# The end of a fused attention and expert kernel: where the last group's sums are read, and where the closing products stand

## The chip, the cores and the metric

The kernel runs on one core of one Trainium2 chip. A core has five engines that run side by side and wait for each other through semaphores: TensorE (PE; its weight loads are shown apart as PEld), VectorE (DVE), ScalarE (ACT), GpSimd (POOL), and SyncE (SP), which issues DMAs. PE multiplies into PSUM, eight banks of 128 partitions x 512 floats; DVE and ACT read and write PSUM and SBUF; POOL works in SBUF alone. The metric is the device time of one launch in microseconds (us), lower is better.

## The reference

Two blocks follow each other. The first is an attention with polynomial features: with `phi(x)` the 64 products of two 8-wide projections of `x`,

```python
kv  = einsum('bhsf,bhsd->bhfd', phi(k), v);  z = sum(phi(k), axis=2)
out = einsum('bhsf,bhfd->bhsd', phi(q), kv) / (einsum('bhsf,bhf->bhs', phi(q), z) + 1e-6)
```

Its result, as 4352 tokens of width 128, is `x` of the second block, a layer of eight experts with Sinkhorn routing:

```python
P = exp(x @ w_gate - max)                 # 4352 x 8
for _ in range(8):                        # rows, then columns, then N / E
    P /= P.sum(1); P /= P.sum(0); P *= N / E
for e in range(8):
    out += P[:, e:e+1] * (relu(x @ w1[e]) @ w2[e])   # w1: 128 x 1024, w2: 1024 x 128
```

Everything is in 32-bit floats.

## The kernel before

The attention and the routing take the first part of the span; most of the rest are the experts' two products. They are computed on 64x64 blocks with seven products in place of eight for each 2x2 block product, so that a weight tile of PE is 64x64 and four of them lie in the array at once: two row halves (`r`, where the input lies) by two column halves (`s`, where the output goes). The weight of a token is multiplied into its input ahead of the first product, which is allowed because it is positive and the Relu lets it through.

**Tokens and units.** The first 256 tokens (`REST`) are handled by themselves. The other 4096 are eight groups of 512 (`wgroups`, line 929). Seven experts by eight groups are 56 items (`witems`), each of two halves of the hidden width: 112 units (`units`). A unit has, for each row half, seven first products (`first_product`, line 1082), copies, sums and the Relu on ACT and DVE (`taps`, `hsums`), and seven second products, the tasks 0 to 6 of `second_products` (line 1123). Two records of the profile make one 64-wide matmul instruction, and a task has two such instructions, one for each `s`.

**The sums.** A group's second products add up over its seven experts in four PSUM banks, `ysums[g][0..3]`, tiles `s`. Bank `2 * r` holds two pieces of 256 columns, slots 0 and 1; bank `2 * r + 1` holds slots 2 and 3. Tasks 0 and 1 write slot 0, tasks 2 and 3 slot 1, tasks 4 and 5 slot 2, task 6 slot 3. For the last unit the tasks run in the order 6, 0, 4, 5, 1, 2, 3 (line 1321): banks 1 and 3 are complete first, then slot 0 of banks 0 and 2, and slot 1 last. What this file calls the two-piece bank is bank 0, read by the copy of line 1227.

**The order of the work** is written out by hand. `weighted_events` (line 1288) gives every instruction of this part a key, `b` plus an offset with `b = 14 * k` for unit `k`; the calls are made in the order of the keys, and each engine runs its own instructions in that order. Waits follow from which tile an instruction reads or writes. A PSUM tile is tracked as a whole: a write to one half of a bank waits for an earlier read of the other half.

**The last group's sums** (`last_end`, line 1204) are formed in 21 steps with the offsets `LAST_AT` (line 1202), behind unit 111, the last one. Steps 0 and 1 copy bank 1 to SBUF on ACT and add bank 3 on DVE; steps 2 and 3 move halves to the other partitions on ACT (lines 1220, 1221); steps 4 to 8 are DVE additions. Step 9 copies slot 0 of bank 0 (line 1227, ACT), step 10 adds slot 0 of bank 2 (DVE), steps 11 and 12 move halves (lines 1229, 1230, ACT), steps 13 to 16 are DVE additions, 17 and 18 add the slots 1 of banks 0 and 2 straight from PSUM. Step 19 transposes (line 1282, DVE) and step 20 stores (line 759, two DMAs from SP and two from POOL). All DVE additions have the line of the helper, 1216.

**The closing products** are the last expert's for the first 256 tokens, unsplit in the row direction: a weight tile of 128 rows by 64 columns (`128*64` in the profile, against `64*64`). `closing_first` (line 1180) makes the hidden part `c` of eight: two matmul instructions into bank `fbanks[c % 3]`, then a Relu on ACT (line 1185). `closing_second` (line 1187) makes one half `b` of 128 tokens of the output: an identity product that brings in what the other experts gave (`c = -1`), then eight products. `closing_out` (line 1195) copies the half to SBUF on ACT and issues four stores, two from SP and two from ACT. In the kernel before, `CLOSING_AT` (line 1167) puts the parts 0 to 3 at the offsets 24, 27, 30 and 33, among the second products of unit 110, and 4 to 7 behind everything of the last unit; both halves of the output use one bank, `fbanks[3]`.

```python
    LAST_AT = (42.1, 42.6, 42.7, 42.8, 43, 43.1, 43.2, 43.3, 43.4, 44.1, 44.6, 44.7, 44.8, 44.9, 45, 45.1, 45.2, 47.1, 47.6, 48.1, 48.2)
...
                for n, key in enumerate(CLOSING_AT):
                    at(b + key, closing_first, n)
                for n in range(2):
                    for c in range(-1, FO):
                        at(b + 49 + n, closing_second, n, c)
                    at(b + 49 + n, closing_out, n)
```

## Time and profile before

| what | value |
|---|---|
| timed runs, median of 3 | 909.7 us (908.74 to 910.84) |
| profiled execution | 907.8 us |
| its span, first to last instruction | 905.8 us |
| mean granted clock of PE | 0.995 |
| PE busy | 896.1 us of the span |
| first of the records of line 1183 | 880.3 us |
| copy of bank 1 (line 1218) starts | 887.71 us |
| last copy to SBUF (second line 1197) starts | 902.26 us |

In a timeline row stand the start in us, the busy time, the engine (a q behind it: its sequencer, as for a DMA issue), the line, the operation, what is written and read, the shape, the number of records, and in brackets the idle time of that engine just before and who ended it. A row of merged records lasts from the start of its first to the end of its last. In a chain row stand start, length, engine, tile, line and count. The granted clock is the share of PE's full speed that it was allowed; records take twice as long at 0.50. Matmul records overlap, since several tiles lie in the array at once.

### The profile page before, as it was taken

Reading aid. Unit: us, or ns where it says so; the run is one execution under the profiler, and the core shown is the slowest. Engines: PE = TensorE matmul, PEld = TensorE weight load, DVE = VectorE, ACT = ScalarE, POOL = GpSimd, SP = SyncE. Lnnn points to the kernel's source line nnn. Section 1 sums busy time; section 2 is a strip of 40 time slices with the busy share of each in tenths; the row PEclk is TensorE's granted clock in tenths of the full one; section 3 lists DMA queues with packets and bytes.
Section 4 is the critical chain, followed back from the end, with each engine's and each line's share of the span. In section 5 each row is a group of like instructions: output and inputs, shape, how many; then the busy total and the mean of one; then the engine's idle time right before and its main releaser. Section 6 shows DMA issues by size and latency. Waiting matters only on the chain.

```text
span 905.8 us, 34686 instructions
## 1 busy us (share of the span) xinstructions
PE 896.1 (99%) x14680; PEld 720.3 (80%) x14680; DVE 744.0 (82%) x1170; ACT 527.7 (58%) x1281; POOL 362.3 (40%) x373
## 2 busy tenths in 40 slices
PE   9999999999999999999999999999999999999997
PEld 6786667688787777788789998888888888878874
DVE  8667678968988988899898878887997898888862
ACT  3353456466566665665666566666656665666652
POOL 3013310042443535465763455354435443643310
PEclk9999999999999999999999999999999999999998
DMA  9998492235568877777886677787767777776710
GB/s 261 311 269 263 148 321 79 65 141 145 179 217 255 234 194 221 210 228 223 232 238 200 199 216 215 213 233 219 211 186 218 224 204 221 222 229 187 220 53 18
DMA packets 149498, 183.97 MB, mean 203 GB/s; under 512 B 15392, under 2 KB 111664, under 8 KB 148960
## 3 DMA queue, kind: packets, MB, share of 16 engines
q1 hardware_dynamic: 144048, 164.24, 62.0%
q0 software_dynamic: 4960, 17.42, 5.6%
q8 instruction: 116, 1.90, 0.8%
q14 instruction: 38, 0.31, 0.1%
q10 hardware_dynamic: 336, 0.10, 0.0%
HBM read 148.38 MB, written 18.65 MB: 184 GB/s over the span
## 4 chain that ended last, share of the span: by engine, by line
PE 95%; DVE 3%; issue 1%; ACT 1%; DMA 1%; SPq 0%; POOL 0%; ACTq 0%; DVEq 0%; POOLq 0%
PE a L1086 37%; PE s L1136 36%; PE a L789 8%; PE s L853 7%; PE a L371 1%; PE s L868 1%; PE a L486 1%; PE a L119 1%; PE a L1183 1%; PE a L1190 0%; PE a L338 0%; DVE hb L1115 0%; PE s L400 0%; PE a L450 0%; DVE hb L1121 0%
## 5 line engine op out<-in xcount | busy, mean ns | idle before, releaser
L1086 PE MATMUL a<-wb,w1f 64*64 64x256 f32 x4144 | 430.9, 377 | 0.4
L1086 PEld LDWEIGHTS a<-wb,w1f 64*64 64x64 f32 x4144 | 271.4, 133 | 36.2 <-issue 3.2
L1086 PE MATMUL a<-xf,w1f 64*64 64x256 f32 x2128 | 230.4, 377 | 0.3 <-DVE ht L1107 0.3
L1100 ACT COPY a<-a 128x256 f32<-128x256 f32 x224 | 80.0, 357 | 213.4 <-PE a L1086 213.4
L1136 PE MATMUL s<-hb,w2r 64*64 64x256 f32 x1344 | 191.2, 379 | 2.5 <-ACT wb L1227 2.1
L1136 PE MATMUL s<-ht,w2r 64*64 64x256 f32 x1344 | 190.4, 376 | 0.0
L201 POOL TENSOR_TENSOR wb<-wb 128x256 f32<-128x256 f32 (+1 forms) x115 | 131.0, 1141 | 118.7 <-DMA wb<-wb 91.8
L1136 PE MATMUL s<-ht,w2f 64*64 64x256 f32 x1216 | 159.5, 376 | 0.0
L1136 PE MATMUL s<-hb,w2f 64*64 64x256 f32 x1216 | 158.8, 377 | 0.0
L1086 PEld LDWEIGHTS a<-xf,w1f 64*64 64x64 f32 x2128 | 142.9, 133 | 18.5 <-issue 1.3
L1136 PEld LDWEIGHTS s<-hb,w2r 64*64 64x64 f32 x1344 | 113.0, 134 | 24.0 <-ACT wb L1227 2.5
L1136 PEld LDWEIGHTS s<-ht,w2r 64*64 64x64 f32 x1344 | 113.6, 133 | 18.9
L1136 PEld LDWEIGHTS s<-ht,w2f 64*64 64x64 f32 x1216 | 99.1, 133 | 8.4
L791 ACT ACTIVATE hb<-a 128x256 f32<-128x256 f32 (+3 forms) x144 | 63.2, 445 | 72.9 <-PE a L789 69.9
L1136 PEld LDWEIGHTS s<-hb,w2f 64*64 64x64 f32 x1216 | 98.5, 133 | 8.5 <-issue 1.2
L789 PE MATMUL a<-xT,wb 128*64 128x416 f32 (+3 forms) x448 | 104.3, 459 | 0.0
L853 PE MATMUL s<-hb,wb 128*64 128x416 f32 (+3 forms) x408 | 100.7, 453 | 0.0
L201 POOL TENSOR_TENSOR xf<-xf 128x256 f32<-128x256 f32 (+1 forms) x62 | 72.2, 1167 | 68.3 <-DMA xf<-xf 43.8
L201 POOL TENSOR_TENSOR wb<-wb,xT 128x512 f32<-128x512 f32 x37 | 51.3, 1386 | 101.7 <-DMA wb<-pT 74.5
L1107 DVE TENSOR_TENSOR ht<-a,mid 128x256 f32<-128x256 f32 x112 | 47.2, 421 | 49.1 <-ACT a L1095 38.1
L1095 ACT COPY a<-a 128x256 f32<-128x256 f32 x224 | 80.0, 357 | 9.3 <-PE a L1086 1.1
L1098 ACT COPY mid<-a 128x256 f32<-128x256 f32 x224 | 84.7, 378 | 0.0
(212 smaller groups left out, 1655.1 us busy)
## 6 DMA issues: line engine op xcount, KB each, us to landing
w1f<-packed SPq DMA_DIRECT2D x204, 224.0 KB, 5.2
w2r<-in_moe_w_dram SPq DMA_DIRECT2D x56, 512.0 KB, 7.1
w2f<-packed SPq DMA_DIRECT2D x68, 256.0 KB, 4.6
wb<-pT SPq DMA_DIRECT2D x45, 256.0 KB, 4.5
wb<-wb SPq DMA_DIRECT2D x74, 128.0 KB, 3.9
hb<-packed SPq DMA_DIRECT2D x32, 256.0 KB, 6.2
xf<-pT SPq DMA_DIRECT2D x19, 256.0 KB, 4.3
xf<-xf SPq DMA_DIRECT2D x36, 128.0 KB, 4.3
```

The lines of the kernel that those rows point to most:

```text
L119: nc.tensor.matmul(warm[:, 0:P], ones, ones, start=True, stop=True)
L201: tc.keep_in_program_order(nc.gpsimd.tensor_tensor(*args, op=op))
L371: nc.tensor.matmul(pv[64 * s:64 * (s + 1), i], kp[0:n, H * t + h].rearrange("p i j -> p (i j)"), vx[0:n, slots[h], t, :], start=(t == 0 an ...
L789: nc.tensor.matmul(ph[sl], loaded_w[items[j][1]][0][:, P * f + H2 * s:P * f + H2 * (s + 1)], xT[:, lo:hi], start=True, stop=True, tile_pos ...
L791: nc.scalar.activation(out=out, in_=ph, func=Act.Relu)
L853: nc.tensor.matmul(sums[g][i][H2 * s:H2 * (s + 1)], w, x, start=c == 1, stop=c == per, tile_position=(0, H2 * s))
L1086: nc.tensor.matmul(half_of(r, b, c, n)[rows[s]], w1s[i][rows[r], 1 + form, u, H2 * s:H2 * (s + 1)], xf(i, x)[rows[r]], start=m == opens, s ...
L1095: nc.scalar.copy(b, a)
L1098: nc.scalar.copy(m5s[k, r], c)
L1100: nc.scalar.copy(d, a)
L1107: nc.vector.tensor_tensor(h[:, H3, r], d, m5s[k, r], op=Alu.add)
L1136: nc.tensor.matmul(place[rows[s]], w[form][rows[r], pair, u], h[rows[r], x, pair], start=task in (0, 4) and k in firsts, stop=True, tile_p ...
```

## The change

Three things, all in the last 26 us.

- `CLOSING_AT`: the closing parts 0 to 3 stand together at offset 34, behind the second products of unit 110 and ahead of those of unit 111.
- `LAST_AT` and `last_end`: step 9 copies both slots of bank 0 (512 columns in place of 256) and stands at 46.1, behind the last write to that bank; the later steps follow at 47.1 to 47.95. The two additions that read slot 1 come two places sooner, the first of them from the copy.
- `closing_second` and `closing_out`: half `b` uses the first 128 columns of bank `fbanks[3 - b]`, so the two halves no longer share a bank, and each opens its own sum.

```diff
-    CLOSING_AT = (24, 27, 30, 33, 48, 48.2, 48.4, 48.6)
+    CLOSING_AT = (34, 34, 34, 34, 48, 48.2, 48.4, 48.6)
...
-            nc.tensor.matmul(fbanks[3][rows[s], P * b:P * (b + 1)],
+            nc.tensor.matmul(fbanks[3 - b][rows[s], 0:P],
...
-                             ident if c < 0 else closing_w[1][:, c], start=c < 0 and not b, stop=True,
+                             ident if c < 0 else closing_w[1][:, c], start=c < 0, stop=True,
...
-        nc.scalar.copy(y, fbanks[3][:, P * b:P * (b + 1)])
+        nc.scalar.copy(y, fbanks[3 - b][:, 0:P])
...
-    LAST_AT = (..., 43.4, 44.1, 44.6, 44.7, 44.8, 44.9, 45, 45.1, 45.2, 47.1, 47.6, 48.1, 48.2)
+    LAST_AT = (..., 43.4, 46.1, 47.1, 47.2, 47.3, 47.4, 47.5, 47.6, 47.7, 47.75, 47.8, 47.9, 47.95)
...
-         lambda: nc.scalar.copy(z[:, 0], s[0][:, 0]),
+         lambda: nc.scalar.copy(z[:, 0:2], s[0]),
          lambda: add(z[:, 0], z[:, 0], s[2][:, 0]),
          lambda: nc.scalar.copy(x[upper, 1], z[lower, 0]),
          lambda: nc.scalar.copy(x[lower, 1], z[upper, 0]),
          lambda: add(y[:, 1], y[:, 1], z[:, 0]),
          lambda: add(y[lower, 0], z[lower, 0], k[lower, 0]),
+         lambda: add(y[:, 0], y[:, 0], z[:, 1]),
+         lambda: add(y[:, 0], y[:, 0], s[2][:, 1]),
          lambda: add(y[upper, 0], y[upper, 0], x[upper, 1]),
          lambda: add(y[:, 1], y[:, 1], x[:, 1]),
-         lambda: add(y[:, 0], y[:, 0], s[0][:, 1]),
-         lambda: add(y[:, 0], y[:, 0], s[2][:, 1]),
```

More of the change, by code (lines that the diff above doesn't have):

```diff
@@ L1200, in closing_out @@
                                                   in_=y[32 * a:32 * (a + 1)])
-    LAST_AT = (42.1, 42.6, 42.7, 42.8, 43, 43.1, 43.2, 43.3, 43.4, 44.1, 44.6, 44.7, 44.8, 44.9, 45, 45.1, 45.2, 47.1, 47.6, 48.1, 48.2)
+    LAST_AT = (42.1, 42.6, 42.7, 42.8, 43, 43.1, 43.2, 43.3, 43.4, 46.1, 47.1, 47.2, 47.3, 47.4, 47.5, 47.6, 47.7, 47.75, 47.8, 47.9, 47.95)
     def last_end(g, step):
```

## The prediction

> **What bounds the kernel now.** I read the page's busy table and chain first.

> ```profile
> PE 896.1 (99%) x14680; PEld 720.3 (80%) x14680; DVE 744.0 (82%) x1170; ACT 527.7 (58%) x1281; POOL 362.3 (40%) x373
> PE 95%; DVE 3%; issue 1%; ACT 1%; DMA 1%; SPq 0%; POOL 0%; ACTq 0%; DVEq 0%; POOLq 0%
> ```

> TensorE (PE) is the bound from end to end, so an edit of the last 26 us pays only if it changes when PE gets through its last products. Next the waits of PE alone, from 880 us on (engine, line, whom it waited for: total, times, longest):

> ```profile
> PE s L1136 <- ACT wb L1227: 2.1, 1, 2.1
> PE s L1136 <- DVE wb L1216: 0.5, 1, 0.5
> PE a L1190 <- ACT mid L1197: 0.4, 1, 0.4
> ```

> These are the three places that the change aims at, 3.0 us together. Their price is higher than that, as PE's granted clock shows, here in stretches of 3.41 us (length, PE busy, matmul records, clock, DMA share, GB/s):

> ```profile
> 10.01:13.42 3.41, 2.78 (x76) 1.00 1.09 381
> ...
> 887.23:890.64 3.41, 1.34 (x22) 1.00 0.00 0
> 890.64:894.05 3.41, 2.94 (x14) 0.50 0.01 2
> 894.05:897.47 3.42, 3.42 (x18) 0.50 0.27 54
> 897.47:900.88 3.41, 3.04 (x54) 1.00 0.15 29
> ```

> After a stretch with 1.34 us of work in it (2.07 idle) the clock is halved, for exactly two stretches. One with 0.63 idle, at 10 us, cost nothing. The first halved stretch, 2.94 busy, did not bring the full clock back; the second, wholly busy, did. The end in order of time:

> ```profile
> 887.71 0.59 ACT L1218 COPY wb<-s 128x512 f32<-128x512 f32 x1 [1.49 <-PE s L1136]
> ...
> 889.77 0.36 ACT L1227 COPY wb<-s 128x256 f32<-128x256 f32 x1
> 890.18 1.56 PE L1136 MATMUL s<-hb,w2r 64*64 64x256 f32 x8 [2.07 <-ACT wb L1227]
> 890.37 0.42 DVE L1216 TENSOR_TENSOR wb<-wb,w 128x256 f32<-128x256 f32 x1 [0.45 <-ACT wb L1227]
> ...
> 891.74 0.42 DVE L1216 TENSOR_TENSOR wb<-wb,s 128x256 f32<-128x256 f32 x1
> 892.20 0.40 ACT L1229 COPY w<-wb 64x256 f32<-64x256 f32 x1 [2.06 <-DVE wb L1216]
> ...
> 892.22 1.97 PE L1136 MATMUL s<-hb,w2r 64*64 64x256 f32 x8 [0.47 <-DVE wb L1216]
> ...
> 892.62 0.40 ACT L1230 COPY w<-wb 64x256 f32<-64x256 f32 x1
> ...
> 894.12 3.58 PE L1183 MATMUL a<-kept,kept 128*64 128x256 f32 x16
> ...
> 894.75 0.71 DVE L1282 STREAM_TRANSPOSE mid<-wb 128x512 f32<-128x512 f32 x1
> 895.28 0.38 ACT L1185 ACTIVATE ht<-a 128x256 f32<-128x256 f32 x1 [2.26 <-PE a L1183]
> 895.49 0.90 SPq L759 DMA_DIRECT2D out_dram<-mid  x2
> ...
> 897.75 1.91 PE L1190 MATMUL a<-kept,ht 128*64 128x128 f32 x32
> 899.71 0.27 ACT L1197 COPY mid<-a 128x128 f32<-128x128 f32 x1 [1.58 <-PE a L1190]
> 900.03 0.44 PE L1190 MATMUL a<-ident,kept 128*64 128x128 f32 x4 [0.37 <-ACT mid L1197]
> 900.30 1.92 PE L1190 MATMUL a<-kept,ht 128*64 128x128 f32 x32
> 902.26 0.27 ACT L1197 COPY mid<-a 128x128 f32<-128x128 f32 x1 [2.29 <-PE a L1190]
> ```

> The reader is to see that each step is released by the one before it, and that the 16 records at 894.12 run in the halved clock. I number the eight first closing products c0 to c7.

> **The change, part by part.** The sum is made against the profiled execution: 907.8 us, of which 905.8 are its span. It lies 1.9 below the median of the timed runs, 909.7, to which I apply the same difference.

> *c0 to c3 in one block.* The chain of waits in order of time:

> ```profile
> 860.97 0.43 PE a L1086 x8
> ...
> 880.40 0.58 PE a L1183 x4
> 880.98 1.01 PE s L1136 x12
> 881.99 0.58 PE a L1183 x4
> ...
> 885.20 0.58 PE a L1183 x4
> 885.78 1.90 PE s L1136 x32
> ```

> From 880.40 to 885.78, 5.38 us, PE does four closing products (16 records, array tiles of 128*64) and 40 records of the unit before the last (64*64). In the steady part 8 records take 0.43, so 40 take 2.15; a closing product takes 3.58/4/2 = 0.45 at full clock, four 1.79. That is 3.94; the other 1.44 is four round trips between tilings, 0.36 each. One round trip is left: 4.30, **1.1 us less**. Part of the 1.44 is that the pieces between the closings do not load both halves of the array alike; that goes too, and the gain is 1.4 at most; if the block brought its own stalls, nothing. I take 1.2, near the lower of the two counts. No operand is late, although PE now comes to the products that were behind c0 to c2 up to 2.7 us sooner, and to the last unit 1.2 sooner, at 884.6:

> ```profile
> 877.75 1.28 POOL L201 TENSOR_TENSOR hb<-hb 128x512 f32<-128x512 f32 x1 [15.48 <-DVE hb L1118]
> ...
> 881.02 0.39 ACT L1185 ACTIVATE ht<-a 128x256 f32<-128x256 f32 x1 [0.85 <-PE a L1183]
> 882.19 0.69 DVE L1121 TENSOR_TENSOR hb<-hb 128x512 f32<-128x512 f32 x1
> ```

> POOL's difference is there at 879.03 and the last one of DVE at 882.88. c3 reuses c0's bank: c0's Relu ended at 881.41, 1.0 after c0 began, and c3 comes 1.35 after c0. So this stays covered by 0.3.

> *Reading the two-piece bank behind all products.* PE runs the last unit's 14 pieces through: 32 records in 1.90, then 24 at the steady pace, 1.29. They end at 884.6 + 3.2 = 887.8, not at 894.19. The waits of 2.07 and 0.47 are gone. The copy L1227 is of 512 instead of 256 columns, 0.59 (as L1218) for 0.36. Its wait for the last lower-half products is hidden: ACT, busy with L1221, comes to it some 0.8 later than they end. The additions are as many as before; one reads a copy in place of the bank, at 0.42 either way.

> *What is late next.* c4 to c6 start at once: 887.8 + 0.2 (half a round trip) + 3 x 0.45 = 889.3. c7 writes the bank of c4 and needs c4's Relu. On ACT that Relu stands behind L1229 and L1230, which wait for DVE's addition at 891.74. This **new wait** holds on ACT the four Relus, and on PE c7 and, behind it, the 72 records of both closing halves. Its end: L1218 starts 1.2 sooner, at 886.5; L1230 ended 893.02 - 887.71 = 5.31 after that start; the wider copy adds 0.23, since DVE went on at 890.37 only behind L1227 (if it waited in truth for L1221, nothing is added). L1230 ends at 886.5 + 5.3 + 0.2 = 892.0, the Relu 0.4 later, c7 starts at 892.4. PE is idle from 889.3 to 892.4, **3.1 us** (2.8 to 3.2), more than the 2.07 before.

> *The second half in a bank of its own.* The 0.37 goes. Behind c7's start, at full clock: c7 0.45, a half of 36 records 1.95, the second half to its copy 902.26 - 900.03 = 2.23; in all 4.6. The last copy starts at 897.1, not 902.26: **5.2 us sooner at full clock**.

> *The clock.* A gap of 2.07 in one stretch halved it; 3.1 should. I take the stretches' grid as not tied to the program, which one trace cannot show. If a boundary falls late in the gap, the clock is halved from there for 6.83, of which 4.4 to 6.8 lie on work: cost 2.2 to 3.4. If it falls up to 1.3 behind c7's start, with enough of the gap ahead of it, halved time is 3.41 (if one wholly busy stretch releases it) or 6.83 (as here), cut off by the end of the work: 1.7 to 3.3. From 5.2 that leaves 1.8 to 3.5; I take **2.5**, near the middle of it: span 903.3, execution 905.3, median 907.2.

> *The stores.* The last group's transpose starts at 894.75 - 1.2 + 0.2 = 893.8, and its stores are issued from 894.5. SP's queue holds behind them the four of the closing halves; the first half's copy is there about 895 to 897, so they wait under 0.5, beside PE's work. POOL has nothing behind its two stores.

> ```profile
> out_dram<-mid SPq DMA_DIRECT2D x2, 64.0 KB, 3.9
> out_dram<-mid ACTq DMA_DIRECT2D x4, 16.0 KB, 1.6
> ```

> In the built program SP's first store of the second half waits for the semaphore of SP's first group store: 894.5 + 3.9 = 898.4. In the forecast the copy is there at 899.8, so this costs nothing; at full clock it would.

> **Rivals.** *The clock stays full.* Then PE's gain is 5.2, but the stores at 898.4 take over from the copy's 897.4. From the first of these issues (902.53 before) to the span's end were 3.3, so 901.6: gain 4.2, median **905.5**. It needs the gap to lie across two stretches so that neither has as much idle time as halves the clock; that amount is between 0.63 and 2.07, and with 3.1 of idle time few positions do it. [...]

> *The half clock lasts.* Release took a wholly busy stretch, and the one in which c7 starts is not. If the clock falls at c7's start and the release is late, all 4.4 us of work left double: gain 0.8, median **908.9**, not to be told from none (0.2%, 1.8 us, is about what a measurement of this kernel can tell).

> *Slower.* The half clock of before cost some 2.8 (6.83 halved, less the waits in it). If the timed runs of before mostly escape it, because their 2.07 lies across two stretches, while the 3.1 of the changed kernel never does, my 2.5 becomes -0.3 and the 0.8 above becomes -2.0: **911.7**. It decides only where both hold. For it speaks that the timed runs spread over 2.1 us; against it, that they all lie above the profiled one, in which the clock did fall.

> That the change is without effect is excluded by the built order: PE waits for neither ACT nor DVE inside the last pieces, and L1227 is 512 wide.

> **How the numbers follow.** Halved clock in the gap or just behind it 0.60, full clock 0.19, lasting half clock 0.15, slower 0.06. The likeliest gives 907.2. The range takes in the full clock with half a microsecond of spread, 904.9, and the lasting half clock, 909.2. Faster by over 0.2%: 0.19 and nearly all of the 0.60, together 0.76; within: 0.18; slower: 0.06.

> **What would show it.** Right: no wait of PE at L1136 behind 885; one PE wait of about 3 us before the last L1183 pair, released by ACT L1185; the pieces of L1183 at 880 to 885 in one run of 16 records; L1218 at about 886.5; a stretch of clock 0.50 over most of L1190; no wait between the halves. Wrong: clock 1.00 at the end (the first rival), L1218 no earlier (the block gains nothing), a wait of PE for c3's bank, or SP's last stores as the end of the chain.

## The result, and the profile after

The changed kernel takes **904.8 us** (median of five runs, 903.37 to 906.80) where the kernel before takes 909.7 (908.74 to 910.84). The ratio is 0.9949, with a 95% interval of 0.9931 to 0.9967: some 4.6 us gained, nearly twice the 2.5 forecast. The profiled execution took 903.37 us, with a span of 901.3.

The page of the changed kernel, busy time of TensorE (PE) and the shares of the chain that ended last:

```profile
PE 888.9 (99%) x14680; PEld 724.2 (80%) x14680; DVE 740.9 (82%) x1170; ACT 527.5 (59%) x1281; POOL 360.7 (40%) x373
...
PE 94%; DVE 2%; DMA 1%; issue 1%; ACT 1%; SPq 0%; ACTq 0%; DVEq 0%
```

The same 14680 records kept PE busy 7.2 us less. By the rows of before, about 3.2 us of that is the clock (2.94 + 3.42 us busy in its two halved stretches); the rest is work that now overlaps more, in the block and in the last pieces. The waits of PE from 878 us on are one row in place of three, and the stretches of the clock's grid show where it fell (PE busy, records, granted clock, DMA share, GB/s):

```profile
PE a L1183 <- ACT ht L1185: 2.9, 1, 2.9
```

```profile
888.58:891.99 3.41, 1.58 (x16) 1.00 0.01 2
891.99:895.40 3.41, 2.35 (x39) 1.00 0.02 5
895.40:898.81 3.41, 2.24 (x42) 1.00 0.47 97
```

```profile
902.23:903.62 1.39, 0.00 (x0) 0.50 0.02 6
```

The last row lies behind the end of the span, when PE has nothing left to do; it shows where the grid stands, and counting back from 902.23 by 3.41 gives the three stretches above. The gap of 2.9 us lies across two of them, 1.83 in the first and the rest in the second, and the clock stayed at 1.00 through both. The end in order of time, ahead of it one row of the kernel before that the prediction did not need:

```profile
877.92 0.42 DVE L1107 TENSOR_TENSOR hb<-a,mid 128x256 f32<-128x256 f32 x1 [0.34 <-PE a L1086]
```

```profile
878.97 0.42 DVE L1107 TENSOR_TENSOR hb<-a,mid 128x256 f32<-128x256 f32 x1 [0.34 <-PE a L1086]
...
883.53 1.95 PE L1183 MATMUL a<-kept,kept 128*64 128x256 f32 x16
...
887.40 0.59 ACT L1218 COPY wb<-s 128x512 f32<-128x512 f32 x1 [1.49 <-PE s L1136]
...
887.62 1.09 PE L1136 MATMUL s<-hb,w2r 64*64 64x256 f32 x16
...
888.64 1.52 PE L1183 MATMUL a<-kept,kept 128*64 128x256 f32 x12
...
889.47 0.57 ACT L1227 COPY wb<-s 128x512 f32<-128x512 f32 x1
890.07 0.42 DVE L1216 TENSOR_TENSOR wb<-wb,w 128x256 f32<-128x256 f32 x1 [0.46 <-ACT wb L1227]
...
892.32 0.40 ACT L1230 COPY w<-wb 64x256 f32<-64x256 f32 x1
892.63 0.91 ACT L1185 ACTIVATE ht<-a 128x256 f32<-128x256 f32 x3
...
893.05 0.65 PE L1183 MATMUL a<-kept,kept 128*64 128x256 f32 x4 [2.90 <-ACT ht L1185]
...
895.72 0.27 ACT L1197 COPY mid<-a 128x128 f32<-128x128 f32 x1 [1.58 <-PE a L1190]
...
897.68 0.27 ACT L1197 COPY mid<-a 128x128 f32<-128x128 f32 x1 [1.70 <-PE a L1190]
```

L1107 at 877.92 and at 878.97 is the same instruction of unit 110 in the two kernels, just ahead of the first edit: the profiled execution of the changed kernel came there 1.05 us later. It lagged by 1.28 us within its first 12 us already, far ahead of every edit. So the tail is compared from there:

| stage of the profiled execution | before | after | gained |
|---|---|---|---|
| L1107 to copy L1218 | 9.79 | 8.43 | 1.36 |
| L1218 to the last copy L1197 | 14.55 | 10.28 | 4.27 |
| last copy to the end of the span | 3.54 | 3.62 | -0.08 |
| sum | 27.88 | 22.33 | 5.55 |

Less the late start of 1.05 that is the 4.5 by which the spans differ. It was not all runs that kept the full clock, though: of the first five, two had a mean granted clock of 1.000 (spans 901.3 and 902.5) and three 0.998 (903.0, 904.2 and 905.0). One stretch of 3.41 at half clock gives that mean (3.41 x 0.5 / 903 = 0.0019); no run of this kernel at 0.998 was profiled, so where its stretch lies is not seen.

### The profile page after: what moved, and what is told of

Its sections match the earlier page's. It is cut to its first block, busy times and chain, and to the rows that moved or that the text cites. A ratio compares the mean times of both kernels' runs of the same rounds, so it can differ in the third digit from the quotient of the medians.

```text
span 901.3 us, 34685 instructions
## 1 busy us (share of the span) xinstructions
PE 888.9 (99%) x14680; PEld 724.2 (80%) x14680; DVE 740.9 (82%) x1170; ACT 527.5 (59%) x1281; POOL 360.7 (40%) x373
## 4 chain that ended last, share of the span: by engine, by line
PE 94%; DVE 2%; DMA 1%; issue 1%; ACT 1%; SPq 0%; ACTq 0%; DVEq 0%
PE a L1086 37%; PE s L1136 36%; PE a L789 8%; PE s L853 7%; PE a L371 1%; PE s L868 1%; PE a L486 1%; DMA kx<-in_k_dram 1%; PE a L338 0%; PE a L1190 0%; DVE hb L1115 0%; PE s L400 0%; DMA xd<-xt 0%; PE a L450 0%; DVE ht L1107 0%
## 5 line engine op out<-in xcount | busy, mean ns | idle before, releaser
L1086 PE MATMUL a<-wb,w1f 64*64 64x256 f32 x4144 | 430.8, 377 | 0.5 <-DVE ht L1107 0.5
L1086 PEld LDWEIGHTS a<-wb,w1f 64*64 64x64 f32 x4144 | 274.7, 133 | 33.4 <-issue 2.5
L1086 PE MATMUL a<-xf,w1f 64*64 64x256 f32 x2128 | 229.8, 377 | 0.7 <-DVE ht L1107 0.5
L1136 PE MATMUL s<-ht,w2r 64*64 64x256 f32 x1344 | 191.5, 377 | 0.0
L1136 PE MATMUL s<-hb,w2r 64*64 64x256 f32 x1344 | 189.1, 376 | 0.0
L201 POOL TENSOR_TENSOR wb<-wb 128x256 f32<-128x256 f32 (+1 forms) x115 | 131.8, 1148 | 119.4 <-DMA wb<-wb 94.0
L1136 PE MATMUL s<-ht,w2f 64*64 64x256 f32 x1216 | 159.4, 376 | 0.0
L1136 PE MATMUL s<-hb,w2f 64*64 64x256 f32 x1216 | 157.8, 376 | 0.0
L1086 PEld LDWEIGHTS a<-xf,w1f 64*64 64x64 f32 x2128 | 142.6, 133 | 17.8 <-POOL wb L201 1.6
L1136 PEld LDWEIGHTS s<-ht,w2r 64*64 64x64 f32 x1344 | 114.1, 133 | 18.0 <-DVE ht L1121 0.3
L1136 PEld LDWEIGHTS s<-hb,w2r 64*64 64x64 f32 x1344 | 113.4, 133 | 17.5 <-DVE hb L1121 0.2
L1136 PEld LDWEIGHTS s<-ht,w2f 64*64 64x64 f32 x1216 | 99.8, 133 | 7.5
L1136 PEld LDWEIGHTS s<-hb,w2f 64*64 64x64 f32 x1216 | 98.9, 133 | 7.5 <-issue 0.4
L201 POOL TENSOR_TENSOR xf<-xf 128x256 f32<-128x256 f32 (+1 forms) x62 | 70.4, 1138 | 71.2 <-DMA xf<-xf 51.2
L201 POOL TENSOR_TENSOR wb<-wb,xT 128x512 f32<-128x512 f32 x37 | 50.1, 1354 | 101.1 <-DMA wb<-pT 64.7
L1107 DVE TENSOR_TENSOR ht<-a,mid 128x256 f32<-128x256 f32 x112 | 47.3, 422 | 52.5 <-ACT a L1095 40.5
```

What stands on the lines that cost most here:

```text
L201: tc.keep_in_program_order(nc.gpsimd.tensor_tensor(*args, op=op))
L1086: nc.tensor.matmul(half_of(r, b, c, n)[rows[s]], w1s[i][rows[r], 1 + form, u, H2 * s:H2 * (s + 1)], xf(i, x)[rows[r]], start=m == opens, s ...
L1107: nc.vector.tensor_tensor(h[:, H3, r], d, m5s[k, r], op=Alu.add)
L1136: nc.tensor.matmul(place[rows[s]], w[form][rows[r], pair, u], h[rows[r], x, pair], start=task in (0, 4) and k in firsts, stop=True, tile_p ...
```

## The experiments

The theory held at first was that of the prediction: the gap in PE's work sets off the half clock, by the idle time that one stretch of the grid holds. The rival was that something else in a stretch counts. The first four runs asked what the gap costs and what the clock does, the next three what each part of the change does alone, the last four what the clock goes by and what sets the end.

**before_again and after_again**: both kernels unchanged, for more runs and profiles.

> The kernel before, once more, for the granted clock of each of its runs. Theory (the clock is judged in stretches of 3.41 us on a grid of its own; a stretch with about 2 us or more without PE work halves it for the next ones): the 2.07 us gap lies whole in one stretch in some 4 of 10 runs and is split in the others, so the mean granted clock should differ between runs: about 0.995 where halved, 0.998 or more where not, and the halved runs are 2 to 3 us longer. Rival (the gap halves the clock whatever the grid): 0.995 in every run, and run-to-run differences have nothing to do with the clock.

> The changed kernel, once more. Theory: its 2.9 us gap in front of the last closing product of the first layer is split harmlessly in about 3 runs of 10; these have a clock of 0.998 to 1.000 and spans near 901.3, the others are halved (0.995 to 0.998) and 1.7 to 3.4 us longer. Ratio to before 0.995 (0.993 to 0.997). Rival (the new gap never halves the clock): clock 0.998 or more and the same span within 1 us of each other in all runs.

Before: 909.62 us, ratio 1.0007 (0.9994 to 1.0020), and in its 12 runs and all 61 others of it that stood beside the experiments the clock was 0.995 to 0.998, never 1.000: the share of runs that were to escape the halving did not come. After: 904.83, ratio 0.9951 (0.9938 to 0.9964), three of six runs at 1.000 and three at 0.998. With the first five that makes five runs of eleven at full clock, mean span 902.4, and six at 0.998, mean span 903.6. So the half clock costs the changed kernel about 1.2 us in about half of its runs, where 1.7 to 3.4 were expected, in seven of ten. The 1.2 is an estimate: within each of the two groups the spans scatter over 2.6 to 3.1 us. The kernel before lost the full clock in every run. The second profile of the changed kernel has its gap elsewhere in the grid:

```profile
888.98:892.39 3.41, 2.45 (x32) 1.00 0.01 2
892.39:895.81 3.42, 1.49 (x24) 1.00 0.02 5
895.81:899.22 3.41, 3.10 (x58) 1.00 0.44 89
```

1.93 us idle in one stretch, and still the full clock behind it.

**relu_ahead**: the Relus and products c4 to c7 stand ahead of the copies L1229 and L1230 in program order.

```diff
-    CLOSING_AT = (34, 34, 34, 34, 48, 48.2, 48.4, 48.6)
+    CLOSING_AT = (34, 34, 34, 34, 47.11, 47.12, 47.13, 47.14)
```

> The changed kernel with the last four closing products and their Relus called ahead of steps 11 and 12 of the last group's sums, so that ACT no longer holds the Relus behind two copies that wait for DVE. Theory: PE's gap of 2.9 us shrinks to 0.5 or less, c7 starts near 890.4 in place of 893.05, PE ends about 2.6 us sooner, and the clock is never halved before the end: clock 0.998 or more in all runs. The end is then set by SP, which issues the last group's stores (from 895.3) ahead of the closing ones: the span ends near 900.5, 0.8 less than the profiled 901.3, and the median falls by 2 to 3 us against the changed kernel, since no run is halved. Rival (the gap is harmless and the end is set by the group's stores anyway): within 0.8 us of the changed kernel in every run.

903.53 us, ratio 0.9935 (0.9921 to 0.9949). The timeline of this kernel:

```profile
886.15 0.58 ACT L1218 COPY wb<-s 128x512 f32<-128x512 f32 x1 [1.49 <-PE s L1136]
...
888.69 0.91 ACT L1185 ACTIVATE ht<-a 128x256 f32<-128x256 f32 x3
...
889.12 0.65 PE L1183 MATMUL a<-kept,kept 128*64 128x256 f32 x4 [0.21 <-ACT ht L1185]
...
893.35 0.71 DVE L1282 STREAM_TRANSPOSE mid<-wb 128x512 f32<-128x512 f32 x1
893.75 0.27 ACT L1197 COPY mid<-a 128x128 f32<-128x128 f32 x1 [1.70 <-PE a L1190]
...
894.08 0.89 SPq L759 DMA_DIRECT2D out_dram<-mid  x2
894.35 1.29 POOL L759 DMA_DIRECT2D out_dram<-mid  x2 [15.53 <-DVE mid L1282]
895.06 1.85 SPq L1199 DMA_DIRECT2D out_dram<-mid  x4
```

The gap of 2.90 is now 0.21: what held c4's Relu was its place behind the two copies on ACT, as the prediction said. From L1218 the last copy comes after 7.60 us instead of 10.28. But from L1218 to the end of the span are 12.95 (899.1 - 886.15) against 13.90, only 0.95 less. PE and ACT's last copy are done at 894.0, before the last group's transpose is (894.06): the end passes to that group's stores, which DVE's additions release. The timed runs fell by 1.3 us (904.83 to 903.53) where 2 to 3 were expected, and by the intervals that is not clear of the changed kernel. Five of the six had a clock of 0.998 or 0.999; PE is idle here for the last 5 us of the span, so a halving behind its last product can be enough for that. The profile of before shows one: its clock is at 0.50 from 904.29 to the end of the span (1.51 us, with no record of PE in it). In stores_ahead, below, the mean is 0.999 in four of four, some 1.8 us at 0.50 (an estimate: 2 x 0.001 x 899.8); where they lie no row shows.

**gap_filled**: twelve idle products of 64 columns between c6 and c7, into an unused half of a bank; their results are not read.

```diff
+    def filler():
+        for n in range(12):
+            s = n % 2
+            nc.tensor.matmul(fbanks[3][rows[s], REST:2 * REST], closing_w[0][:, H2 * n:H2 * (n + 1)], kept_small[:, E - 2],
+                             start=True, stop=True, tile_position=(0, H2 * s), skip_group_check=True)
...
+                at(b + 48.5, filler)
```

> The changed kernel with 12 idle matmuls (128 rows by 64 columns, 256 wide, into an unused half bank, results not read) between c6 and c7, 2.6 us at full clock, so the wait for c4's Relu stays and ends at the same time, but PE has hardly 0.3 us without work. Theory: c7 starts at the same time as in the changed kernel, and the clock stays full in every run: the median equals the changed kernel's runs with full clock, some 1 to 2 us below its median. Rival (the gap costs only its own length): the same median as the changed kernel, or slightly more.

904.16 us, ratio 0.9938 (0.9923 to 0.9952); by time alone it can't be told from the changed kernel, but the clock was 1.000 in all six runs (changed kernel: five of eleven). The wait left, in its timeline:

```profile
891.56 2.76 PE L1190 MATMUL a<-kept,kept 128*64 128x256 f32 x24
894.63 0.65 PE L1183 MATMUL a<-kept,kept 128*64 128x256 f32 x4 [0.30 <-ACT ht L1185]
```

The end of the wait is not moved by work in the gap: c7 starts 14.08 us behind L1107 in both kernels (894.63 - 880.55; 893.05 - 878.97). And no run here has the half clock.

**block_only, read_behind_only, own_banks_only**: one part each. The first is the kernel before with the new `CLOSING_AT`; the second the changed kernel with the other two parts undone; the third the kernel before with `closing_second` and `closing_out` of the change.

```diff
-    CLOSING_AT = (24, 27, 30, 33, 48, 48.2, 48.4, 48.6)
+    CLOSING_AT = (34, 34, 34, 34, 48, 48.2, 48.4, 48.6)
```

> The kernel before with only the first four closing products moved together. Theory (six changes of the array's tiling and some unbalanced pieces go): from the last unit's first sums on DVE to the copy L1218 1.36 us less than before (9.79 there, 8.43 in the changed kernel); 1.1 to 1.4 us less in all, ratio 0.9987, if the clock behaves as before. Rival (PE was waiting there for the sums of DVE and POOL, so the block only moves the wait): L1218 at the same time, no gain.

> The kernel before with only the two-piece bank read behind all products, and the later steps moved. Theory: the waits of 2.07 and 0.47 go, and a new one of 2.9 us appears before c7, released by ACT L1185; c4 to c6 run ahead of it, and the last copy starts some 3.6 us sooner at full clock (4.27 from L1218 in the changed kernel, less 0.37 for the shared bank and 0.3 for the restart); ratio 0.997 to 0.995 with some runs halved. Rival (the gain came from the block and the banks): 1 us or less.

> The kernel before with only a bank of its own for each closing half. Theory: the wait of 0.37 and the restart behind it go, the second half follows the first without a break: 0.3 to 0.5 us less, ratio 0.9995, not to be told from 1. Rival (the second half's stores or the copy are what ends last): nothing.

| kernel | us | ratio (95%) | clock of its runs |
|---|---|---|---|
| block_only | 907.82 | 0.9985 (0.9971 to 0.9999) | 0.995 to 0.998 in 12 of 12 |
| read_behind_only | 907.27 | 0.9974 (0.9961 to 0.9986) | 1.000 in 4 of 11, else 0.998 |
| own_banks_only | 909.51 | 1.0005 (0.9992 to 1.0019) | 0.994 to 0.998 in 12 of 12 |

The block gives its 1.36 (L1107 at 880.51 to L1218 at 888.94 in this profile is 8.43 as in the changed kernel) and nothing else. The two kernels that keep the waits inside the last pieces lost the full clock in every run; the one that gathers the idle time into one gap kept it in 4 of 11. A mean below 1.000 does not say where the clock fell: the profile of own_banks_only has, beside the stretches in the tail, one at half clock from 37.74, in the attention, and none of the other twelve profiles does. The profile of read_behind_only is of a run that lost the clock. Its wait is the expected one, 2.89 us in front of c7, and this is where the clock fell:

```profile
892.95:896.36 3.41, 1.33 (x20) 1.00 0.03 7
896.36:899.77 3.41, 3.05 (x30) 0.50 0.39 76
```

From L1218 to the last copy it took 12.27 us (901.65 - 889.38) against 14.55 in before: 2.28 less, not the 3.6 forecast for full clock. From c7's start to that copy were 6.62 (901.65 - 895.03); the changed kernel takes 4.63 and a shared bank 0.59 more (2.55 - 1.96, below), so the halved stretch cost 1.4 in this run.

The banks alone take the wait between the halves away, from 2.55 us between the two copies of before to 1.96:

```profile
906.43 0.27 ACT L1197 COPY mid<-a 128x128 f32<-128x128 f32 x1 [2.00 <-PE a L1190]
...
908.39 0.27 ACT L1197 COPY mid<-a 128x128 f32<-128x128 f32 x1 [1.70 <-PE a L1190]
```

Those 0.6 us are too few to be told from the scatter of the timed runs. The three parts sum to 0.15 + 0.26 - 0.05 = 0.36% beside the 0.5% of all together; the intervals cover the difference.

block_only shows what the idle-time theory can't explain. Its timeline and its stretches:

```profile
891.42 1.08 PE L1136 MATMUL s<-hb,w2r 64*64 64x256 f32 x8 [2.06 <-ACT wb L1227]
...
893.45 1.08 PE L1136 MATMUL s<-hb,w2r 64*64 64x256 f32 x8 [0.95 <-DVE wb L1216]
```

```profile
891.00:894.41 3.41, 2.04 (x16) 1.00 0.01 2
894.41:897.83 3.42, 3.42 (x18) 0.50 0.08 14
897.83:901.24 3.41, 3.04 (x54) 1.00 0.37 69
```

1.37 us idle (3.41 - 2.04) halved the clock here, where 1.83 and 1.93 did not in the changed kernel. What PE ran differs: sixteen records on quarters of the array (64*64), all in one row half, in place of twelve that take half of the array each. Eight 64*64 records lay four at a time in 0.43 us in the steady part, so one is worth 0.43/8 = 0.054 us of the whole array, a 128*64 record of 256 columns twice that. By this count, an estimate from these rows, the stretch of block_only holds 16 x 0.054 = 0.86 us, 25% of 3.41; the one of before that halved the clock, 887.23, holds sixteen such records too (by their starts), 25%; the stretch 888.58 of the changed kernel twelve of 0.107, 38%. All records are counted where they start and at their full-clock time, in halved stretches too.

**gap_longer**: c4 and c5 use one bank, so that c5, not c7, waits for c4's Relu, and the gap begins after c4.

```diff
-        ph = fbanks[c % 3][:, 0:REST]
+        ph = fbanks[(0, 1, 2, 0, 1, 1, 2, 0)[c]][:, 0:REST]
```

> The changed kernel with another choice of banks for the last four closing products, so that c5 in place of c7 is the one that waits for c4's Relu: PE's gap grows from 2.9 to 3.8 us, and 0.9 us of work moves behind it. Theory: however the grid lies, one stretch has 1.9 us or more without work, so the clock is halved in nearly every run: clock 0.995 to 0.997, and 0.9 + 1.7 to 3.4 us longer than the full-clock runs of the changed kernel (spans of 903.9 to 905.6). Rival (the clock does not follow the gap): clock as in the changed kernel, 0.9 us longer.

906.59 us, ratio 0.9973 (0.9958 to 0.9989), clock 0.996 to 0.998 in 12 of 12. The median span, 904.6, lies within the 903.9 to 905.6 expected, and no run had the full clock. A gap of 3.75 fills a stretch nearly alone:

```profile
892.08:895.49 3.41, 0.27 (x4) 1.00 0.01 2
895.49:898.90 3.41, 2.79 (x14) 0.50 0.02 5
898.90:902.31 3.41, 3.41 (x67) 1.00 0.42 85
```

The middle row also shows that a stretch need not be wholly busy to bring the full clock back, as the prediction had taken it: 2.79 did.

**longer_filled and longer_small_filled**: that gap filled, once with sixteen products of 64 columns in pairs that use the whole array, once with sixteen of 32 by 32, one after the other, so that PE is just as busy and the array nearly empty. Their results are not read. The two theories part at the second. Its edit, beside that of gap_longer:

```diff
+    def filler():
+        for n in range(16):
+            nc.tensor.matmul(fbanks[3][0:32, REST:2 * REST], closing_w[0][0:32, 32 * n:32 * (n + 1)], kept_small[0:32, E - 2],
+                             start=True, stop=True, tile_position=(0, 0), skip_group_check=True)
...
+                at(b + 48.1, filler)
```

> The longer gap (3.75 us, c5 held) filled with 16 idle 64-column products in 8 pairs, which use the whole array; their results are not read. TensorE's wait of 3.75 shrinks to about 2. Theory A (the clock follows how much of the array is used in a stretch of 3.41 us) and theory B (it follows TensorE's idle time) say the same: clock 1.00 at the end in nearly all runs, where the unfilled longer gap had it below 1.00 in 12 of 12; time about 1.2 us under the unfilled one's 906.6, so 905.4, since the full clock takes its toll away and the filling itself ends before c4's Relu does.

> The same gap filled with 16 products of 32 by 32, one after the other, which keep TensorE busy but use a sixteenth of the array; their results are not read. By the durations of other products they last some 0.21 us each, 3.4 us in all, so that TensorE's idle time in the gap is under 0.5 us. Theory A (array use): the clock still falls, as in the unfilled gap, below 1.00 in nearly all runs, time 906.0 to 907.0. Theory B (idle time): the clock stays at 1.00 and the time is about 905.4, like the filling with whole-array products or better.

Whole array: 905.35 us, ratio 0.9955 (0.9938 to 0.9972), clock 1.000 in four of four; 905.4 was expected. PE's wait shrank to 0.31, not to about 2, since a product lasts twice as long as was reckoned (the sixteen are 32 records, 3.62 us in the trace); c5 still starts 14.09 us behind L1107, as in gap_longer (14.08). Small: 913.11, ratio 1.0050 (1.0031 to 1.0069), clock 0.993 to 0.996 in six of six. The timeline and the stretches of the small filling:

```profile
893.36 0.65 PE L1183 MATMUL a<-kept,kept 128*64 128x256 f32 x4
893.94 9.29 PE L1189 MATMUL a<-kept,kept 32*32 32x256 f32 x32
903.16 2.83 PE L1183 MATMUL a<-kept,kept 128*64 128x256 f32 x12
```

```profile
895.24:898.65 3.41, 3.41 (x17) 1.00 0.01 2
898.65:902.06 3.41, 3.41 (x10) 0.50 0.27 53
902.06:905.48 3.42, 3.42 (x15) 0.50 0.12 24
905.48:908.89 3.41, 3.41 (x34) 0.50 0.00 0
908.89:912.30 3.41, 2.51 (x46) 1.00 0.07 19
```

PE was busy for the whole of the first stretch, with no idle time at all (3.41 of 3.41), and behind it the clock was at 0.50: by idle time it should have stayed at 1.00 here. Sixteen 32*32 records are worth 16 x 0.0134 = 0.21 us of the array, 6%. My expected time was missed because I put such a product at 0.21 us; it is two records of 0.21, so the filling outlasted the gap, the more so at half clock.

**stores_ahead**: relu_ahead, and SP issues the first closing half's stores ahead of the last group's.

```diff
-                        at(b + 49 + n, closing_second, n, c)
-                    at(b + 49 + n, closing_out, n)
+                        at(b + (47.92, 50)[n], closing_second, n, c)
+                    at(b + (47.92, 50)[n], closing_out, n)
```

(and these stores and the last group's are kept in program order).

> The Relus ahead of the moves, and in addition SP issues the first closing half's two stores ahead of the last group's stores. PE, ACT and DVE are unchanged. If SP's queue sets the end (its last store was issued at 896.4 of 899.1), the last issue comes 0.9 us sooner, and the time is about 0.9 under the 903.5 of the Relus ahead of the moves. If the last group's own stores set it (the chain of waits names POOL's), nothing is gained: 903.5.

901.96 us, ratio 0.9924 (0.9903 to 0.9945): faster than both kernels of the study, and by the interval not to be told from relu_ahead. The chain of waits of this profile, from L1218 and at its end:

```profile
886.84 0.59 ACT wb L1218
...
894.01 0.72 DVE mid L1282
894.74 0.28 issue
895.02 0.65 POOL out_dram L759
895.68 0.64 POOLq L1478
```

From L1218 to the span's end, 899.8, are 12.96 us, as in relu_ahead (12.95). So SP's queue was not what ended there; it is the last group's additions, transpose and stores. The second of the two expectations holds, and the 1.6 us by which this median lies below relu_ahead's 903.53 is not a gain of this stage: the spans of the two profiles are 899.8 and 899.1.

## Why the prediction was right and where it failed

**The block: right.** Forecast 1.1 to 1.4, taken 1.2; measured 1.36 from L1107 to L1218, in the changed kernel and in block_only. The 1.1 was for three of the four round trips, and one-sided loading of the array was to be worth 0.3 more at most; the 1.36 lies between the two counts, and how it divides no run shows. c3's bank cost no wait.

**The two waits: right, one term too large.** They are gone from the list of waits. The wider copy (0.57 instead of 0.36) was charged 0.23; DVE went on 2.67 us after L1218's start (890.07 - 887.40), as before (890.37 - 887.71 = 2.66). So it had not waited for the copy, and nothing was added, as the bracket in the prediction allowed. The addition reads `w`, which L1221 wrote; that copy had ended 0.51 ahead of it in both kernels, so what released it is not fully shown.

**The new wait: right.** One gap in front of c7, forecast 3.1 (2.8 to 3.2), measured 2.90, released by the Relu; relu_ahead shows that the place on ACT made it. From c7's start to the last copy, forecast 4.6, measured 897.68 - 893.05 = 4.63. The 5.2 sooner at full clock, with the block's 0.16 more and without the 0.23, become 5.6; measured 5.63 (1.36 + 4.27).

**The clock: the step that failed.** "A gap of 2.07 in one stretch halved it; 3.1 should" took idle time as the measure and charged 2.7 of the 5.2. In fact the clock stayed full in 5 of 11 runs; the 6 others lost, by their mean, one stretch, at about 1.2 us (1.4 in the profile of read_behind_only): 0.65 on average. 5.55 - 0.65 = 4.9 is near what the timed runs show (4.5 to 4.6 by the ratios, 4.9 by the first medians). So the direction and the stages were foreseen, but not the size: 904.8 lies 2.4 below the likeliest 907.2, at the very edge of the range (904.9), which reaches there only because it takes in the first rival. That the range holds it is luck as far as the clock goes.

The step was wrong in three places. In these runs the clock went with how much of the array is used, by the count above, and not with idle time: it was at 0.50 behind a stretch with 16 records of a quarter of the array (25%, with 2.07 idle in before and 1.37 in block_only) and behind one of 32*32 products without any idle time (6%), while it stayed at 1.00 behind a stretch with 1.97 idle and 34% of the array's work (before_again 902.31). The 2.07 of before was therefore not a price list for other gaps: its stretch held no more than sixteen quarter records. And release took one stretch behind the single gap, in read_behind_only and gap_longer, whose first halved stretch holds 41% of the array's work by the same count; the first halved one of before, with one-sided pieces and a wait in it, holds 12 quarter records, 19%, and its second was halved too.

**The first rival** (full clock) was what the profiled execution did, and its chance of 0.19 was too low. Its cap was wrong too: SP's second-half stores were to wait for the first group store until 898.4, by a landing of 3.9 us. The table of DMA issues of the changed kernel has

```profile
out_dram<-mid SPq DMA_DIRECT2D x2, 64.0 KB, 2.6
```

so that the wait ended at 895.32 + 2.6 = 897.9, with the copy (897.95), and cost nothing. The gain behind full clock was the 5.55 of the stages, not the rival's 4.2. The length of the longest wait alone does not tell the runs apart: with the gap of 2.9 the clock stayed full in five runs of eleven, but before, with waits of 2.07 and 0.47, had it in none of 73.

Two sums of the prediction are off by 0.1 in the rounding: 892.4 + 4.6 is 897.0, and 905.5 less half a microsecond 905.0.

**The slower rival** needed timed runs of before that escape the halving. None of 73 had the full clock. Its two waits and the one-sided pieces behind them fill some 5 us at full clock (2.06 + 1.08 + 0.95 + 1.08 by the rows of block_only), one and a half stretches with 0.86 us of the array's work in them; that this leaves some stretch poorly used wherever the grid falls is argued from the rows, the 73 runs are measured. That before lost the clock in every run, and the changed kernel in about half, belongs to the gain: the 5.55 is that of a run that kept it against one that did not.

## What to carry to other kernels

Where PE is the bound and must wait, look at the granted clock in stretches and add up what part of the array its products use in each. Two short waits (2.06 or 2.07, then 0.25 to 0.95) with one-sided products between them cost the full clock in all 97 runs of the three kernels that have them (73 of before, 12 each of block_only and own_banks_only); one gap of 2.9 between products of 128*64 in 13 of 22 (the changed kernel and read_behind_only); one of 3.75 in 12 of 12 (gap_longer). The waits removed from PE here moved to whoever was next in line on ACT: order the queue of the engine that releases the bound by who stops the bound (the Relus ahead of the copies gave 2.7 of 2.9 us back). And once PE was through, the other chain to the output became the end: only 0.95 of those 2.7 us reached it.

## What the runs showed of the hardware

| stretch | idle us | use of the array | clock behind it |
|---|---|---|---|
| longer_small_filled 895.24 | 0.00 | 6% | halved |
| block_only 891.00 | 1.37 | 25% | halved |
| before 887.23 | 2.07 | 25% | halved |
| before 900.88 (last work, 20 records) | 2.08 | 31% | halved |
| own_banks_only 34.33 (in the attention) | 1.92 | 32% | halved |
| before_again 902.31 (last work, 22 records) | 1.97 | 34% | full |
| read_behind_only 892.95 | 2.08 | 38% | halved |
| after 888.58 | 1.83 | 38% | full |
| after_again 892.39 | 1.93 | 44% | full |
| longer_small_filled 902.06, halved | 0.00 | 38% | stays halved |
| gap_longer 895.49, halved | 0.62 | 41% | released |
| read_behind_only 896.36, halved | 0.36 | 41% | released |

The same count over the whole of the traces of before and of the changed kernel gives 524 stretches at full clock. Behind three of them, with 0% (after 898.81), 25% and 31%, the clock was at 0.50; behind the other 521, the lowest two of them with 38%, it stayed at 1.00. Of the halved stretches of before the first, with 19%, was followed by another, and the second, with 50%, by the full clock. So the count shows no sharp limit: all five full-clock stretches of the table with up to 32% were followed by the half clock, and of those from 34% to 38% two held and one fell; two stretches with the same 38%, after 888.58 and read_behind_only 892.95, went different ways. The records that lie across a boundary blur the count by a few per cent (two of 128*64 are 6% of a stretch), which may be the reason; it is not shown. Whether falling and coming back go by the same share, and whether rows or columns of the array count more, these runs do not settle either. A second thing: products that all sat in one row half of the array went at half the pace; eight records took 1.08 us there (block_only at 891.42), and sixteen 1.09 where both row halves were in use (the changed kernel at 887.62).
